# A decode attention kernel: two parts of the last V product as loops over a register

## The chip, the cores and the metric

The kernel runs on one core of a Trainium2 chip. The metric is device time in microseconds (us) of one execution, as the median of several runs. A profile is taken of one execution beside them; it lists the engines' instructions with start and length.

## The reference

Two attention blocks A and B, with the same shapes, each for two batches and a single query token. Their outputs are put side by side.

```
B, Sq, D = 2, 1, 640;  H, Sk, Dh = 32, 8192, 192
q      = (x @ wq) as [B, H, 1, Dh]
scores = einsum("bhqd,bhkd->bhqk", q, k_cache) * Dh ** -0.5
o      = einsum("bhqk,bhkd->bhqd", softmax(scores), v_cache)
out    = o as [B, 1, H * Dh] @ wo
result = concatenate([block A, block B], axis=-1)
```

All inputs are bf16. The K and V caches are most of the bytes: 2 blocks x 2 batches x 32 heads x 8192 tokens x 192 x 2 bytes, for K and for V.

## The kernel before

**Units and parts.** The work is cut into 16 units (`NU`) of one batch and 8 heads (`UH`). The K and the V of a unit are laid on 128 partitions, 16 partitions a head, and each partition has 512 tokens (`TP`) of 192 numbers. Each is loaded in three parts (`NCH`), of 170 whole tokens (`TC`) a partition and fragments of the two tokens that lie across the cuts. `big` has three buffers of one part each; the loads of all units go through them in a fixed order from SP's queue (`ld_kv`, L256), each one waiting until the part that was in its buffer is used up.

**A unit.** VectorE multiplies K with the query in place, TensorE sums over the head dimension with an identity matrix (`pe_sum`, `pe_rest`), VectorE reduces what is left. Then come the maximum, the exponential on ScalarE, and `dve_spread`, which writes the probabilities to `pb` as weights for TensorE. The V product of a unit runs on TensorE beside the K work of the next one.

**The V product** (`pe_pv(u, c)`, L450 in before) of part c takes two tokens a time: 85 products (`TC // 2`) with 40 columns of `pb` as weights (LDWEIGHTS, "PEld" in the profile) and 384 numbers of V a partition as the moving side, all added up in the PSUM tile `ops`. After the first of them come one or two small products for the fragments (L456). `pe_l` (L438) ahead of part 0 sums the exponentials.

**Loops.** `_Stream` holds each engine's instructions as a list, with a tag of slot and name; `emit` makes a hardware loop of slots that repeat, with addresses computed from the loop's register (`at`). Before, TensorE has three: two for the q projection (`pe_proj`, L402: 15 passes of five products of 384 columns each) and one for units 1 to 15, whose body has all 255 V products of a unit written out. A loop's own instructions have line L65.

**The tail.** After that loop comes the V product of the last unit, straight, with no K work beside it. What waits for it:
- When its part 0 is done, SP issues the load of A's output weights (`ld_wo`, L256) into that part's buffer; when part 1 is done, it issues B's in five pieces.
- When part 2 is done, VectorE and ScalarE scale the result (L349 to L358), `pe_pl` and `pe_turn` (L462, L471) turn it, and `pe_out` (L484) multiplies it with A's weights (96 products), then, after eight idle products (`pe_idle`, L492), with B's, piece by piece as they land.
- ScalarE and VectorE (L387, L388) write the sums to SBUF, and SP sends them out.

Of the kernel before, what the change touches and what calls it, by code (L numbers as in the profile page):

```python
# [119 lines left out]
def build_kernel(nc, blocks, out):  # L120
# [4 lines left out]
    UH = 8  # L125
    HG = Hn // UH
    NQB = NBLK * B
    NU = NQB * HG
    LASTU = NU - 1
    TP = Sk * UH // 128  # L130
    NCH = 3
    ROW = TP * Dh // NCH
    TC = ROW // Dh
    FR = ROW - TC * Dh
    OFF = (0, Dh - FR, FR)
# [8 lines left out]
    QW = 2 * Dh  # L144
# [3 lines left out]
    MP = HP + UH  # L148
    HM = Hn // 2
    XM = HM - 1  # L150
    PQ0 = -100
    XW = XM + 128
    PO = 128 - UH
    scale = float(Dh) ** -0.5
# [3 lines left out]
    with ExitStack() as es:  # L158
# [10 lines left out]
        pb = sb("pb", [128, TP * UH], BF16)  # L169
# [17 lines left out]
        rc = sb("rc", [UH, 1], F32)  # L187
# [10 lines left out]
        ops = ps("ops", [128, 512], F32)  # L198
# [8 lines left out]
        bufs = [big[:, i * ROW:(i + 1) * ROW] for i in range(NBUF)]  # L207
# [7 lines left out]
        S_pe = _Stream("pe", sem("s_pe"), reg, 1)  # L215
# [20 lines left out]
        buf = {}  # L236
# [43 lines left out]
        def fragments(b, c):  # L280
            if c == 0:
                return [(0, 0, FR, bufs[b][:, ROW - FR:ROW])]
            if c == 1:
                return [(0, FR, Dh, bufs[b][:, 0:Dh - FR]), (1, 0, Dh - FR, bufs[b][:, ROW - (Dh - FR):ROW])]
            return [(1, Dh - FR, Dh, bufs[b][:, 0:FR])]
# [154 lines left out]
        def col(s):  # L440
            return 64 * (s // 8) + 32 * (s % 2) + 8 * (s % 8 // 2)

        def pe_pv(u, c):
            b = buf["v", u, c]

            def fn(eng):
                for j in range(TC // 2):
                    j0 = col(TC * c + 2 * j)
                    last = c == NCH - 1 and j == TC // 2 - 1
                    ins = eng.matmul(ops[0:MP, 0:QW], pb[:, j0:j0 + MP],  # L450
                                     bufs[b][:, OFF[c] + j * QW:OFF[c] + (j + 1) * QW],
                                     start=(c == 0 and j == 0), stop=last, skip_group_check=True)
                    if j == 0:
                        for t, lo, hi, src in fragments(b, c):
                            j0 = col(NCH * TC + t)
                            eng.matmul(ops[0:UH, lo:hi], pb[:, j0:j0 + UH], src, start=False, stop=False,  # L456
                                       skip_group_check=True)
                return ins
            return fn

        def pe_pl(u):
            return lambda eng: eng.matmul(oacc_all[:, 0:Dh], place[:, S_pe.at(UH * u, 128, UH)], o_sb[:],  # L462
                                          start=False, stop=True, skip_group_check=True)
# [50 lines left out]
        for n in range(1, HP + 1):  # L514
            S_pool.add((lambda n: (lambda eng: eng.memset(tri[0:n, n:n + 1], 1.0)))(n),
                       waits=[("tri0",)] if n == 1 else [], sig=("tri",) if n == HP else None)
# [6 lines left out]
        for blk in range(NBLK):  # L523
            for b in range(B):
                S_dve.add(dve_xz(blk, b), waits=[("px",), ("init", 0)], sig=("xz",) if (blk, b) == (1, 1) else None)
        S_dve.add(lambda eng: eng.tensor_reduce(em[:], ident[:].rearrange("p (m t) -> p t m", t=GP), AXL.X, ALU.add),
                  waits=[("id1",)], sig=("em",))
        for i in range(GP):
# [3 lines left out]
                waits=[("em",), ("init", 2)], sig=("esel",) if i == GP - 1 else None)  # L532
        for i in range(HG):
# [3 lines left out]
                waits=[("init", 3)], sig=("onehot",) if i == HG - 1 else None)  # L537
        S_dve.add(lambda eng: eng.tensor_reduce(mask[:], ident[:].rearrange("p (h y) -> p h y", y=16), AXL.X, ALU.add),
                  sig=("mask",))
# [26 lines left out]

        streams = {"pe": S_pe, "dve": S_dve, "act": S_act, "pool": S_pool}
        slots = {e: {} for e in streams}

        def put(eng, slot, name, fn, waits, lag=0):  # L570
            slots[eng].setdefault(slot, []).append((name, fn, [w for w in waits if w is not None], lag))

        for u in range(NU + 1):
            real, old = u < NU, u >= 1
            v = u - 1

            def red(c, k):
                put("dve", u, ("r", c, k), dve_red(u, c, k), [("s", u, c, k), ("sp", u - 1) if u else None])

            def turn_out():  # L580
                put("dve", u, ("rc", -1), dve_rc, [("pv", v, NCH - 1), ("of", v - 1)])
                put("dve", u, ("oh", -1), dve_ohi, [("of", v - 1)])
                put("dve", u, ("os", -1), dve_osum, [("oh", v)])
                put("act", u, ("of", -1), act_of, [("os", v), ("rc", v), ("pl", v - 1)])

            def v_part(c):
                if c == 0:
                    put("pe", u, ("l", -1), pe_l, [("exp", v), ("sp0", v), ("os", v - 1), ("rc", v - 1)])
                put("pe", u, ("pv", c, -1), pe_pv(v, c), [("v", v, c), ("sp", v) if c else None])

            if not real:
                for c in range(NCH):
                    v_part(c)
                turn_out()
                put("pe", u, ("pl", -1), pe_pl(v), [("of", v)])
                continue
            put("dve", u, ("su", 1), dve_su(u + 1), [("q", u)])
            for c in range(NCH):
                if old:
                    v_part(c)  # L600
                for k in range(NSUB):
                    if old and c == NCH - 1 and k == 3:
                        turn_out()
                    w = [("k", u, c), ("qe", u), ("sl", u - 1, NCH - 1) if u and c == 0 else None]
                    put("dve", u, ("m", c, k), dve_mul(u, c, k), w)
                    put("pe", u, ("s", c, k), pe_sum(u, c, k), [("m", u, c, k), prev(u, c, k)])
                    if old and c == NCH - 1 and k == 3:
                        put("pe", u, ("pl", -1), pe_pl(v), [("of", v)])
                    n = NSUB * c + k - 3
                    if n >= 0:  # L610
                        red(n // NSUB, n % NSUB)
                put("pe", u, ("sl", c), pe_rest(u, c),
                    [("m", u, c, NSUB - 1), ("rl", u - 1) if u and c == 0 else None])
            c = NCH - 1
            for k in range(NSUB - 3, NSUB):
                red(c, k)
            put("dve", u, ("rl",), dve_rest, [("sl", u, c)])
            put("dve", u, ("mx",), dve_max, [("rl", u)])
            put("dve", u, ("mp",), dve_mp, [("mx", u), ("ar", u - 1) if u else None, ("negm",)])
            put("dve", u, ("nm",), dve_nm, [("ar", u)])  # L620
            put("dve", u, ("nb",), dve_nb, [("nm", u), ("exp", u - 1) if u else None])
            put("pe", u, ("q", 1), pe_q, [("su", u + 1), ("qe", u)])
            put("pool", u, ("ar",), pool_ar, [("mp", u), ("nm", u - 1) if u else None])
            put("act", u, ("qe", 1), act_q, [("q", u + 1), ("m", u, NCH - 1, NSUB - 1)])
            put("act", u, ("exp",), act_exp, [("nb", u), ("l", v) if u else None])
            g0, g1 = -(-TC // 8), TP // 8
            put("dve", u, ("sp0",), dve_spread([(0, g0), (g1 - 1, g1)]),
                [("exp", u), ("pv", v, NCH - 1) if u else None, ("mask",)])
            put("dve", u, ("sp",), dve_spread([(g0, g1 - 1)]), [])

        def full(name, u):
            lag = name[-1] if name[0] in ("su", "q", "qe", "l", "pv", "rc", "oh", "os", "of", "pl") else 0
            rest_ = name[1:-1] if lag else name[1:]
            return (name[0], u + lag) + rest_

        for e, S in streams.items():
            order = [n for n, *_ in slots[e][1]]
            have = {n for n, *_ in slots[e][0]}
            after = {}
            at = None  # L640
            for n in order:
                if n in have:
                    at = n
                else:
                    after.setdefault(at, []).append(full(n, 0))
            for u in sorted(slots[e]):
                for n, fn, waits, _ in slots[e][u]:
                    S.add(fn, waits=waits, sig=full(n, u), tag=(u, n),
                          pre=after.get(None, ()) if u == 0 and n == slots[e][0][0][0] else (),
                          post=after.get(n, ()) if u == 0 else ())  # L650

# [13 lines left out]
        with nc.Block() as block:  # L665
            @block.sync
            def _(eng):
                S_sp.emit(eng)

            @block.gpsimd  # L670
            def _(eng):
                S_pool.emit(eng)

            @block.vector
            def _(eng):
                S_dve.emit(eng, [(1, NU, 1)])

            @block.scalar
            def _(eng):
                S_act.emit(eng, [(1, NU, 1)])  # L680

            @block.tensor
            def _(eng):
                S_pe.emit(eng, [(PQ0 + 1, PQ0 + HM, 1), (PQ0 + 2 * HM + 1, PQ0 + 3 * HM, 1), (1, NU, 1)])

        for blk in range(NBLK):
            nc.scalar.wait_ge(*reg["odone", blk])
# [49 lines left out]
```

## Time and profile before

| what | value |
|---|---|
| median of 3 runs | 1937.39 us (1936.87 to 1938.21) |
| profiled execution, its own time | 1937.25 us |
| its span in the trace | 1935.4 us |
| TensorE (PE) busy | 1532.6 us, 79% |
| PE weight loads (PEld) busy | 784.1 us |
| VectorE (DVE) busy | 1119.2 us, 58% |
| DMA | 836.94 MB, mean 432 GB/s |

The span runs from the first instruction to the last; the execution's own time has 1.85 us more around it. "Busy" is the union of an engine's instructions. A matmul's length includes its way through the array, so products that follow each other every 0.16 us are listed with 0.33 each. "PEq" or "PEldq" is PE's sequencer, which computes addresses, branches, and hands instructions to the array. "issue" as a releaser means that an engine waited for nothing that the profile shows.

### The profile page before, as it was taken

The numbers are of one execution on the slowest core, as the hardware profiler recorded it, in microseconds if no ns is written. First come the engines' busy times: TensorE is split into PE (matmuls) and PEld (weight loads), VectorE is DVE, ScalarE is ACT, GpSimd is POOL, SyncE is SP. The second block draws the span as 40 slices with busy tenths as digits, with TensorE's granted clock in tenths as the row PEclk, the third lists the DMA queues.
The fourth block names the chain that finished last, engine by engine and source line by source line (L and its number), as shares of the span: only waits on it lengthen the run. The fifth ranks groups of instructions, "written<-read, shape, count | busy, mean of one in ns | idle before, by whom it ended". The sixth has DMA issues, their size and how long they took to land.

```text
span 1935.4 us, 18767 instructions
## 1 busy us (share of the span) xinstructions
PE 1532.6 (79%) x8255; PEld 784.1 (41%) x8256; DVE 1119.2 (58%) x841; ACT 29.6 (2%) x75; POOL 9.4 (0%) x60
## 2 busy tenths in 40 slices
PE   4778787887888778797787878878797777878778
PEld 2334343443434434353343434433343343434435
DVE  0785555846566485546846566485546846565450
ACT  0000000000000000000000000000000000000000
POOL 0000000000000000000000000000000000000000
PEclk9999898898999999999999999999998988999889
DMA  9999999999999999999999999999999999999998
GB/s 412 435 441 434 434 436 433 433 435 433 433 435 433 433 433 433 433 433 435 437 435 435 433 433 433 433 433 433 433 434 437 435 437 433 433 433 436 433 432 380
DMA packets 15147, 836.94 MB, mean 432 GB/s; under 512 B 1688, under 2 KB 1824, under 8 KB 2208
## 3 DMA queue, kind: packets, MB, share of 16 engines
q1 hardware_dynamic: 15136, 836.78, 99.8%
q8 instruction: 9, 0.15, 0.0%
q14 instruction: 2, 0.02, 0.0%
HBM read 836.77 MB, written 0.01 MB: 432 GB/s over the span
## 4 chain that ended last, share of the span: by engine, by line
PE 35%; DMA 34%; DVE 17%; issue 13%; DVEq 0%; POOL 0%; ACT 0%; SPq 0%; ACTq 0%; POOLq 0%
PE ops L450 22%; DMA big<-in_B_k_cache_dram 17%; DMA big<-in_A_k_cache_dram 14%; DVE big L305 12%; PE scps L420 10%; DVE sc L313 3%; DMA big<-in_B_wo_dram 2%; PE scps L402 2%; PE rest L432 1%; DMA pb<-in_B_x_dram 1%; DVE pb L340 1%; DVE rmax L321 0%; POOL mg L346 0%; PE ops L456 0%; DVE o_hi L352 0%
## 5 line engine op out<-in xcount | busy, mean ns | idle before, releaser
L420 PE MATMUL scps<-big,ident 128*128 128x512 bf16 x2880 | 716.5, 408 | 284.0 <-DVE sc L313 268.1
L305 DVE TENSOR_TENSOR big<-big,qt 128x6144 bf16<-128x6144 bf16 (+1 forms) x240 | 847.5, 3548 | 0.0
L450 PE MATMUL ops<-big,pb 128*40 128x384 bf16 x4080 | 710.7, 336 | 0.0
L420 PEld LDWEIGHTS scps<-big,ident 128*128 128x128 bf16 x2880 | 285.1, 103 | 700.6 <-DVE sc L313 332.9
L450 PEld LDWEIGHTS ops<-big,pb 128*40 128x40 bf16 x4080 | 414.5, 103 | 272.3 <-issue 28.9
L303 DVE TENSOR_TENSOR pad<-big,qt 128x128 bf16<-128x128 bf16 (+1 forms) x64 | 11.9, 207 | 633.7 <-DMA big<-in_B_k_cache_dram 341.5
L313 DVE TENSOR_REDUCE sc<-scps 128x32 f32<-128x512 f32 x240 | 161.0, 681 | 31.2 <-PE scps L420 31.2
L340 DVE TENSOR_TENSOR pb<-sc,mask 128x704 bf16<-128x704 f32 (+2 forms) x96 | 76.3, 863 | 14.1 <-ACT sc L367 14.1
L438 PE MATMUL ops<-rs,mask 128*8 128x1 f32 x32 | 3.1, 167 | 84.8 <-DVE pb L340 84.8
L432 PEld LDWEIGHTS rest<-big,ident 128*128 128x128 bf16 x576 | 44.4, 101 | 13.9 <-issue 4.5
L432 PE MATMUL rest<-big,ident 128*128 128x160 bf16 x576 | 49.1, 236 | 0.0
L438 PEld LDWEIGHTS ops<-rs,mask 128*8 128x8 f32 x32 | 1.6, 90 | 88.4 <-DVE pb L340 82.8
L402 PE MATMUL scps<-big,pb 128*128 (+1 forms) x160 | 31.7, 338 | 6.8 <-issue 6.8
L358 ACT ACTIVATE o_sb<-o_hi,rc 8x192 bf16<-8x192 f32 x16 | 7.3, 454 | 1537.2 <-DVE o_hi L355 1537.2
L349 DVE RECIPROCAL rc<-ops 8x1 f32<-8x1 f32 x16 | 2.3, 147 | 41.4 <-PE ops L450 41.4
L295 DVE TENSOR_TENSOR su<-esel,onehot 128x144 bf16<-128x144 bf16 x17 | 5.1, 300 | 35.8 <-PE outps L410 35.8
L402 PEld LDWEIGHTS scps<-big,pb 128*128 (+1 forms) x160 | 15.7, 99 | 22.6 <-issue 15.1
L395 PE MATMUL rest<-ident,pb 4*128 4x4 bf16 x5 | 0.4, 178 | 21.9 <-DMA pb<-in_B_x_dram 21.9
L346 POOL PARTITION_ALL_REDUCE mg<-mp x16 | 5.8, 365 | 1855.2 <-DVE mp L324 1855.2
L317 DVE TENSOR_REDUCE sc<-rest 128x30 f32<-128x480 f32 x16 | 10.5, 657 | 7.3 <-PE rest L432 7.3
L367 ACT ACTIVATE sc<-sc,nb 128x512 f32<-128x512 f32 x16 | 11.5, 721 | 32.8 <-DVE nb L330 32.8
L292 DVE CAST pb<-rest 128x5 bf16<-128x5 f32 x4 | 0.4, 171 | 19.5 <-PE rest L395 19.5
(66 smaller groups left out, 131.5 us busy)
## 6 DMA issues: line engine op xcount, KB each, us to landing
big<-in_B_wq_dram SPq DMA_DIRECT2D x1, 7680.0 KB, 37.4
big<-in_A_wo_dram SPq DMA_DIRECT2D x1, 7680.0 KB, 29.2
big<-in_A_wq_dram SPq DMA_DIRECT2D x1, 7168.0 KB, 20.3
big<-in_B_wo_dram SPq DMA_DIRECT2D x1, 4640.0 KB, 27.7
big<-in_B_wo_dram SPq DMA_DIRECT2D x1, 1760.0 KB, 31.4
big<-in_B_wo_dram SPq DMA_DIRECT2D x1, 800.0 KB, 32.8
big<-in_A_wq_dram SPq DMA_DIRECT2D x1, 512.0 KB, 3.8
big<-in_A_k_cache_dram SPq DMA_DIRECT2D x24, 38.4
```

Source lines behind the costliest of these rows:

```text
L303: eng.tensor_tensor(pad[:, t, lo:hi], src, qt[:, 0, lo:hi], ALU.mult)
L305: return eng.tensor_tensor(t, t, qt[:].broadcast_to([128, size(k), Dh]), ALU.mult)
L313: return lambda eng: eng.tensor_reduce(sc[:, lo:lo + SUB], scps[bank(u, c, k)][:], AXL.X, ALU.add)
L317: eng.tensor_reduce(dst, rest[:, 0:NCH * REST, :].rearrange("p (c t) g -> p c t g", c=NCH), AXL.X, ALU.add)
L340: ins = eng.tensor_tensor(dst[:, lo:hi, a], src[:, lo:hi, a].unsqueeze(3).broadcast_to(shape), mask[:].unsqueeze(1).unsqueeze(1).broadcast ...
L346: return eng.partition_all_reduce(mg[:], mp[:], 128, bass.bass_isa.ReduceOp.max)
L358: return eng.activation(o_sb[:], o_hi[:], ACTF.Identity, scale=rc[:])
L367: return eng.activation(sc[:], sc[:], ACTF.Exp, bias=nb[:], scale=scale, accum_out=rs[:])
L402: ins = eng.matmul(flat[0][:, 0:QW], xz[:, blk, c, S_pe.at(m, 128)], wq_t[blk][:, c, S_pe.at(QW * m, QW, QW)], start=(blk == 0 and m == 0 ...
L420: ins = eng.matmul(scps[bank(u, c, k)][:], ident[:], t[:, :, j * DG:(j + 1) * DG], start=(j == 0), stop=(j == NJ - 1))
L432: ins = eng.matmul(rest[:, lo:lo + n, :], ident[:], src[:, :, j * DG:(j + 1) * DG], start=(j == 0), stop=(j == NJ - 1))
L450: ins = eng.matmul(ops[0:MP, 0:QW], pb[:, j0:j0 + MP], bufs[b][:, OFF[c] + j * QW:OFF[c] + (j + 1) * QW], start=(c == 0 and j == 0), stop= ...
```

## The change

For the last unit alone, parts 0 and 1 of the V product are written as loops. The first product and the fragments of a part stay ahead of its loop (`pe_pv_head`); the other 84 products are 21 passes (`VN`) of four (`VP`). Both operands' addresses are taken from the loop's register: 64 columns of `pb` and 1536 of V a pass. Each pass ends with a semaphore update; who waited for the part's end now waits for that of its last pass. Part 2 and the units in the main loop stay as they were.

```diff
+    PV0 = 1000
+    VP = 4
+    VN = (TC // 2 - 1) // VP
...
+        def pe_pv_head(u, c):
+            b = buf["v", u, c]
+
+            def fn(eng):
+                j0 = col(TC * c)
+                ins = eng.matmul(ops[0:MP, 0:QW], pb[:, j0:j0 + MP], bufs[b][:, OFF[c]:OFF[c] + QW],
+                                 start=(c == 0), stop=False, skip_group_check=True)
+                for t, lo, hi, src in fragments(b, c):
+                    j0 = col(NCH * TC + t)
+                    ins = eng.matmul(ops[0:UH, lo:hi], pb[:, j0:j0 + UH], src, start=False, stop=False,
+                                     skip_group_check=True)
+                return ins
+            return fn
+
+        def pe_pv_pass(u, c, i):
+            b = buf["v", u, c]
+
+            def fn(eng):
+                for n in range(VP):
+                    j = 1 + VP * i + n
+                    ins = eng.matmul(ops[0:MP, 0:QW], pb[:, S_pe.at(col(TC * c + 2 * j), MP, 16 * VP)],
+                                     bufs[b][:, S_pe.at(OFF[c] + j * QW, QW, VP * QW)],
+                                     start=False, stop=True, skip_group_check=True)
                 return ins
             return fn
...
             if not real:
+                put("pe", u, ("l", -1), pe_l, [("exp", v), ("sp0", v), ("os", v - 1), ("rc", v - 1)])
                 for c in range(NCH):
-                    v_part(c)
+                    if c == NCH - 1:
+                        put("pe", u, ("pv", c, -1), pe_pv(v, c), [("v", v, c)])
+                        continue
+                    put("pe", u, ("pvh", c), pe_pv_head(v, c), [("v", v, c), ("sp", v) if c else None])
+                    for i in range(VN):
+                        n = ("pv", c, -1) if i == VN - 1 else ("pvt", c, i)
+                        put("pe", u, n, pe_pv_pass(v, c, i), [])
+                        tags["pe", u, n] = (PV0 + 100 * c + i, ("pvt", c))
...
-                S_pe.emit(eng, [(PQ0 + 1, PQ0 + HM, 1), (PQ0 + 2 * HM + 1, PQ0 + 3 * HM, 1), (1, NU, 1)])
+                S_pe.emit(eng, [(PQ0 + 1, PQ0 + HM, 1), (PQ0 + 2 * HM + 1, PQ0 + 3 * HM, 1), (1, NU, 1)]
+                          + [(PV0 + 100 * c, PV0 + 100 * c + VN, 1) for c in range(NCH - 1)])
```

How TensorE's instructions stand in the tail, first in before, from the sum of the exponentials (L438) to the placing of the result (L462):

```order
L438 MATMUL ops<-rs,mask 8x1
L450 MATMUL ops<-big,pb 40x384
L456 MATMUL ops<-big,pb 8x128
L450 MATMUL ops<-big,pb 40x384 x85
L456 MATMUL ops<-big,pb 8x64 x2
L450 MATMUL ops<-big,pb 40x384 x85
L456 MATMUL ops<-big,pb 8x128
L450 MATMUL ops<-big,pb 40x384 x84
L462 MATMUL oall<-o_sb,place 128x192
```

There 84 products of part 0 and the first of part 1 stand in a row, then the fragments, and the same again for parts 1 and 2. After the change, TensorE's loop of part 0 (ISA is an address step on PE's sequencer; lines from L110 on are later in the file than before):

```order
L65 UNCONDITIONAL_BRANCH
L65 ISA
L485 ISA
L485 MATMUL ops<-big,pb 40x384
L485 ISA
L485 MATMUL ops<-big,pb 40x384
L485 ISA
L485 MATMUL ops<-big,pb 40x384
L485 ISA
L485 MATMUL ops<-big,pb 40x384
L65 REGISTER_ALU
L65 COMPARE_AND_BRANCH
```

The 84 products have become one body of four that is passed 21 times, with an address step ahead of each and three sequencer steps a pass. The end of the second loop on TensorE and what follows it, after the change:

```order
L65 REGISTER_ALU
L65 COMPARE_AND_BRANCH
L454 MATMUL ops<-big,pb 40x384
L460 MATMUL ops<-big,pb 8x128
L454 MATMUL ops<-big,pb 40x384 x84
L492 MATMUL oall<-o_sb,place 128x192
```

Part 2 (L454, L460) is as it was, and stands right behind the loop's branch.

More of the change, by code (lines that the diff above doesn't have):

```diff
@@ L151, in build_kernel @@
     PQ0 = -100
+    PV0 = 1000
+    VP = 4
+    VN = (TC // 2 - 1) // VP
+    assert VP % 4 == 0 and 1 + VN * VP == TC // 2
     XW = XM + 128
@@ L459, in pe_pv @@
             return fn
+        def pe_pv_head(u, c):
[18 more added lines that the diff above has]
+                                     start=False, stop=True, skip_group_check=True)
+                return ins
+            return fn
         def pe_pl(u):
@@ L568, in build_kernel @@
         slots = {e: {} for e in streams}
+        tags = {}
         def put(eng, slot, name, fn, waits, lag=0):
@@ L647, in build_kernel @@
                 for n, fn, waits, _ in slots[e][u]:
-                    S.add(fn, waits=waits, sig=full(n, u), tag=(u, n),
+                    S.add(fn, waits=waits, sig=full(n, u), tag=tags.get((e, u, n), (u, n)),
                           pre=after.get(None, ()) if u == 0 and n == slots[e][0][0][0] else (),
```

## The prediction

> **What bounds the kernel now.** I read the page's head first, then the chain that ended last, then the tail of the timeline.
>
> ```profile
> span 1935.4 us, 18767 instructions
> PE 1532.6 (79%) x8255; PEld 784.1 (41%) x8256; DVE 1119.2 (58%) x841; ACT 29.6 (2%) x75; POOL 9.4 (0%) x60
> DMA packets 15147, 836.94 MB, mean 432 GB/s; under 512 B 1688, under 2 KB 1824, under 8 KB 2208
> ```
>
> 836.94 MB at 432 GB/s is the whole span: up to the last unit the loads are the bound, and TensorE waits for data. The change touches nothing there. It sits in the last 67 us, where the chain of waits (start, length, what) reads:
>
> ```profile
> 1869.26 15.33 PE ops L450 x85
> ...
> 1884.74 13.77 PE ops L450 x84
> ...
> 1898.53 0.33 SPq L256
> ...
> 1899.38 32.77 DMA big<-in_B_wo_dram
> ...
> 1932.19 1.46 PE scps L484 x16
> ...
> 1933.68 0.48 DVE pb L388
> ```
>
> The two V parts of the change (L450) stand on the chain themselves. The end of part 1 releases SP's issue of the second weight matrix (L256), its landing releases the last output products (L484), and these end the kernel. The timeline of the same stretch shows how much slack the neighbours have:
>
> ```profile
> 1869.19 15.40 PE L450 MATMUL ops<-big,pb 128*40 128x384 bf16 x85
> ...
> 1871.73 0.16 PEld L450 LDWEIGHTS ops<-big,pb 128*40 128x40 bf16 x1 [0.16 <-issue]
> 1872.05 12.14 PEld L450 LDWEIGHTS ops<-big,pb 128*40 128x40 bf16 x75 [0.16 <-issue]
> 1884.45 0.33 SPq L256 DMA_DIRECT2D big<-in_A_wo_dram  x1
> ...
> 1898.53 2.24 SPq L256 DMA_DIRECT2D big<-in_B_wo_dram  x5
> ...
> 1898.74 13.83 PE L450 MATMUL ops<-big,pb 128*40 128x384 bf16 x84
> 1912.60 0.16 DVE L349 RECIPROCAL rc<-ops 8x1 f32<-8x1 f32 x1 [41.44 <-PE ops L450]
> ...
> 1915.58 8.36 PE L484 MATMUL outps<-big,oT 128*2 128x320 bf16 x96
> ...
> 1924.10 1.67 PE L492 MATMUL ops<-big,ident 128*128 128x512 bf16 x7 [0.16 <-issue]
> ...
> 1926.27 5.69 PE L484 MATMUL scps<-big,oT 128*2 128x320 bf16 x80 [0.50 <-DMA big<-in_B_wo_dram]
> ...
> 1932.19 1.45 PE L484 MATMUL scps<-big,oT 128*2 128x320 bf16 x16 [0.23 <-DMA big<-in_B_wo_dram]
> ```
>
> PE has no hole from 1869.19 to 1912.60, and the last output products wait for the DMA by only 0.50 and 0.23 us. DMA and PE end almost together, so whatever lengthens PE's V product moves the end after about a microsecond.
>
> **What a looped pass costs.** No product goes away. 168 of the 255 straight V products become two loops of 21 passes with four products each. A pass adds four address instructions (one ahead of each product), a register step, a branch, and one more address instruction behind the branch. Before has a loop of the same build: the q projection (L402), 15 passes of five products with the same 384 columns.
>
> ```profile
> L402 PEldq FUSED_REGOPS  x150: 42/74/84, 23.1 to 60.3; - x150
> ...
> L65 PEldq COMPARE_BRANCH  x45: 83/215/238, 23.9 to 1862.3; - x45
> ```
>
> Minimum, median and maximum in ns: 150 address instructions (one a product) of 74 ns, and a taken branch of 215 ns, all on PE's sequencer. What they do to the products stands in the timeline of PE and of its weight loads:
>
> ```profile
> 22.78 6.49 PE L402 MATMUL scps<-big,pb 128*128 128x384 bf16 x30 [0.53 <-issue]
> ...
> 29.52 0.73 PEld L402 LDWEIGHTS scps<-big,pb 128*128 x5 [0.53 <-issue]
> ```
>
> ```profile
> 30.79 0.98 PE L402 MATMUL scps<-big,pb 128*128 x5 [0.27 <-issue]
> 32.05 0.98 PE L402 MATMUL scps<-big,pb 128*128 x5 [0.28 <-issue]
> ...
> 40.88 3.50 PE L402 MATMUL scps<-big,pb 128*128 x20 [0.26 <-issue]
> 44.64 0.98 PE L402 MATMUL scps<-big,pb 128*128 x5 [0.26 <-issue]
> ...
> 59.78 0.50 PE L402 MATMUL scps<-big,pb 128*128 x2 [0.27 <-issue]
> ```
>
> ```profile
> 34.00:38.00 4.00, 3.17 (x17) 1.46 (x16) 0.00 (x0) 0.00 (x0) 0.00 (x0) 1.00 1.13 492
> ```
>
> From 30.79 to 59.78 lie 23 passes: 28.99 / 23 = 1.260 us for five products, though at the full clock (1.00 in the third fence's window) a straight product needs 12.14 us / 75 = 0.162 (weight loads from 1872.05), so 0.81 for five. Nothing is waited for ("issue"): the sequencer paces the loop. Within a pass the weight loads follow each other by (0.73 - 0.10) / 4 = 0.158 us, 0.10 being one load; between passes PE's weight loader idles 0.53. So a pass of four is 1.260 - 0.158 = 1.10 us against 4 x 0.162 = 0.65 straight. This value I take. Its bounds from the same rows: 1.26 if the fifth product was free beside the sequencer, 1.26 x 4/5 = 1.01 if everything scales. The step from one loop to the next costs a pass: 40.88 to 44.64 is three passes of 1.25, though five straight products and a loop entry lie in it.
>
> **Part 0.** Before: first product of the 84 at 1869.19, issue of A's weights at 1884.45. After: the 21st pass starts at 1869.19 + 20 x 1.10 = 1891.19, its fourth product 3 x 0.158 later at 1891.67, and with 0.34 for the product itself the issue comes at 1892.0, 7.6 us late. The cold start of before (0.32 us apart until 1872.05, about nine products) does not come on top: 4 x 0.32 = 1.28 lasts three passes at most, and the sequencer is ahead of PE by then, as in the 30 gapless products from 22.78. At most 0.4 us. What hides the late issue is the V part 2 load ahead of it in the queue:
>
> ```profile
> big<-in_A_wo_dram SPq DMA_DIRECT2D x1, 7680.0 KB, 29.2
> ...
> big<-in_A_wq_dram SPq DMA_DIRECT2D x1, 512.0 KB, 3.8
> ```
>
> The last column is us from issue to landing. 7680 KB (7.86 MB) at 432 GB/s are 18.2 us, so of A's 29.2 us 11.0 are spent behind V part 2, until 1884.45 + 11.0 = 1895.5. The first load of all took 3.8 us of which 1.2 move 512 KB, so a start costs at most 2.6: 1892.0 + 2.6 = 1894.6 is still in time. Cost nothing; A lands at about 1913.7 as before.
>
> **Part 1.** Its first pass starts one pass after loop 0's last: 1869.19 + 21 x 1.10 = 1892.29; its 21st at 1914.29, last product 0.48 later, done at 1915.1. There the five DMAs of B's weights are issued, 16.6 us later than 1898.53. Now the cover is gone: A has landed at 1913.7, the DMA engines run dry for about 4 us, and B (7680 KB too) lands at 1915.1 + 2.6 + 18.2 = 1935.9 at the latest.
>
> **Part 2 and the tail.** Part 2 stays straight: 14.07 us from 1898.53 to 1912.60, so the reciprocal comes at 1929.2, and with some 0.1 for leaving the loop 1929.3, 16.7 late. Everything to the eighth idle product moves along; before, that one ended at 1924.10 + 8 x 0.214 = 1925.8, now at 1942.5 (0.214 is 1.67 less the 0.38 of the last, over six steps). B has then been in SBUF for 6.6 us, so the last 96 products run without a wait: 40 pairs took 5.69 with 0.1 of waiting and a last one of 0.30, thus 0.136 a pair, 48 pairs 6.5, and 0.2 until the last is read. They end at 1949.2 instead of 1933.65 (1932.19 + 1.45), 15.5 later: the 16.7 less 1.2 of waits for B that vanish. Behind them nothing changes. Fewer fetches of instructions (320 instructions fewer) weigh nothing where PE is the bound. The gate on PE's clock can add or take one slow window:
>
> ```profile
> 1916.00:1920.00 4.00, 4.00 (x40) 2.19 (x36) 0.00 (x0) 0.00 (x0) 0.00 (x0) 0.57 0.94 408
> ```
>
> Clock 0.57 after the 3 us pause around 1914 cost output products some 1.7 us; I leave it in, as the pause stays.
>
> The profiled execution took 1937.25 us for its 1935.4 span, 0.14 under the median of 1937.39. 1937.25 + 15.5 = 1952.8 us, 0.8% slower. Each 0.01 us on a pass is 0.41 us here.
>
> **Rivals.**
> The other side, *the sequencer runs ahead*: if PE's queue held enough products, the address work would be hidden and nothing moves. For it: 30 products from 22.78 to 29.3 without a gap. Against it: those began at half clock, and when the lead was spent every one of 23 passes showed the gap. It decides below a pass of 0.82 us: the tail may then slip by 1.2 + 3.9 (0.2% of the time, about what a measurement of this kernel can tell from no change) = 5.1 against 16.7, and 11.6 / 41 = 0.28 off 1.10. Fully hidden it gives 1936 to 1937. Chance 5%.
> *Only the branch shows*: address instructions lie beside the products, and a pass costs 0.65 + 0.215 = 0.865. Shift 16.7 - 41 x 0.235 = 7.1, less 1.2: 1943.1 us. Against it: 0.53 of idling where the branch explains 0.215. Chance 4%.
> The Trainium skill, "Advanced Engine Details and Errata", section "Control Flow Timing", states about 108 ns for a compare-and-branch; by that alone an estimated pass is 0.76 us and the time about 1939. The row says 215 for a taken one, and the measurement decides.
> *The clock halves in the loops*: PE's array works 0.65 of each 1.10. If the gate closed, four products at 0.32 make 1.28 a pass: 41 x 0.18 = 7.4 more, 1960.2. Against it: clock 1.00 through the five-product loop, at 0.81 of 1.26. Chance 4%.
> *B's landing ends it*: 6.6 us too early for that; 1%.
>
> **How the numbers follow.** The likeliest, with 86%, is 1952.8. The range takes a pass from 1.00 to 1.20, that is -4.1 to +4.1, with a little below for a sequencer that is quicker when no profile is taken: 1948.0 to 1957.0; the upper bound of 1.26 (1959.4) I leave out, because the spacing of loads shows each product costing its 0.158. Faster by over 0.2%: 1%, since the DMA floor leaves nothing to win. Within 0.2%: 4%. Slower: 95%.
>
> **What would show it.** In the profile after: L485 products in groups of four, 1.10 us apart, with 0.4 us of "issue" between; A's issue near 1892, B's near 1915; a dent in GB/s near 1916; the reciprocal near 1929; last products without a DMA wait. The prediction is wrong if the passes come closer than 0.82 us, or if TensorE's clock in the loops is not 1.00.

## The result and the profile after

The changed kernel took 1952.76 us (median of 6 runs, 1950.94 to 1954.72), the kernel before 1937.16 us (6 runs, 1936.75 to 1938.21). The ratio is 1.0081, 95% interval 1.0068 to 1.0094: 0.8% slower.

The profiled execution took 1954.72 us, the longest of its six. The head of its page, to be held against that of before:

```profile
span 1953.0 us, 19063 instructions
PE 1544.1 (79%) x8255; PEld 784.2 (40%) x8256; DVE 1119.6 (57%) x841; ACT 29.6 (2%) x75; POOL 9.4 (0%) x60
```

The engines do the same work (x8255 products in both); 296 more instructions pass through the sequencers, and the span is 17.6 us longer. The tail of its timeline (start, length, engine, what, count, idle before it and its releaser), TensorE first and then the rows of other engines and the end:

```profile
1870.89 4.92 PE L485 MATMUL ops<-big,pb 128*40 x20
1876.08 0.86 PE L485 MATMUL ops<-big,pb 128*40 x4 [0.28 <-issue]
1877.21 0.82 PE L485 MATMUL ops<-big,pb 128*40 x4 [0.28 <-issue]
...
1892.85 0.86 PE L485 MATMUL ops<-big,pb 128*40 x4 [0.28 <-issue]
...
1894.13 0.83 PE L485 MATMUL ops<-big,pb 128*40 x4
1895.21 0.82 PE L485 MATMUL ops<-big,pb 128*40 x4 [0.25 <-issue]
...
1916.47 0.82 PE L485 MATMUL ops<-big,pb 128*40 x4 [0.32 <-issue]
```

```profile
1893.74 0.33 SPq L260 DMA_DIRECT2D big<-in_A_wo_dram  x1
...
1917.33 2.59 SPq L260 DMA_DIRECT2D big<-in_B_wo_dram  x5
...
1931.47 0.16 DVE L353 RECIPROCAL rc<-ops 8x1 f32<-8x1 f32 x1 [58.61 <-PE ops L454]
...
1934.44 8.36 PE L514 MATMUL outps<-big,oT 128*2 128x320 bf16 x96
...
1942.96 1.67 PE L522 MATMUL ops<-big,ident 128*128 128x512 bf16 x7 [0.16 <-issue]
...
1944.56 6.68 PE L514 MATMUL scps<-big,oT 128*2 128x320 bf16 x96
```

Three things are to be seen here. The looped products come in fours, with 0.28 us of "issue" between: 15 passes from 1876.08 to 1892.85 are 1.118 us each. The issue of B's weights has moved from 1898.53 to 1917.33. And the last 96 output products run in one row without a wait for B, where before they stood in two with waits: the last piece of B's weights landed at 1939.21 us in the trace, and the first of these products starts at 1944.56. TensorE ends this kernel alone.

The clock that was granted to TensorE in the two loops, and the load between them, stand in the windows (the last three numbers are the clock, the busy share of the DMA engines, and GB/s):

```profile
1884.00:1892.00 8.00, 6.00 (x30) 2.79 (x30) 0.00 (x0) 0.00 (x0) 0.00 (x0) 1.00 0.96 418
...
1896.00:1912.00 16.00, 11.58 (x58) 5.38 (x57) 0.00 (x0) 0.00 (x0) 0.00 (x0) 1.00 0.98 426
1912.00:1916.00 4.00, 3.12 (x16) 1.50 (x16) 0.00 (x0) 0.00 (x0) 0.00 (x0) 1.00 0.04 15
```

The clock was full (the first loop's first 2.6 us, up to 1873.5, were at half clock, as the start of this tail was in before), and behind A's weights the DMA engines ran dry.

The whole tail of this execution lies 1.70 us later than that of before from its first product on (L442 at 1870.13 against L438 at 1868.43), and this lateness arises ahead of the changed code: the tails of e1 and e4, which have loops too, start at 1868.46 and 1868.40 (see the section on the hardware). Where start times are compared below, they are taken from the tail's own start.

### The profile page after: what moved, and what is told of

It is laid out like the page before. It is cut to its first block, busy times and chain, and to the rows that moved or that the text cites. A ratio compares the mean times of both kernels' runs of the same rounds, so it can differ in the third digit from the quotient of the medians.

```text
span 1953.0 us, 19063 instructions
## 1 busy us (share of the span) xinstructions
PE 1544.1 (79%) x8255; PEld 784.2 (40%) x8256; DVE 1119.6 (57%) x841; ACT 29.6 (2%) x75; POOL 9.4 (0%) x60
## 4 chain that ended last, share of the span: by engine, by line
PE 35%; DMA 34%; DVE 18%; issue 13%; DVEq 0%; POOL 0%; ACT 0%; SPq 0%; ACTq 0%; POOLq 0%
PE ops L454 20%; DMA big<-in_A_k_cache_dram 19%; DMA big<-in_B_k_cache_dram 14%; DVE big L309 13%; PE scps L424 9%; DVE sc L317 3%; PE ops L485 2%; PE scps L406 2%; PE rest L436 1%; DMA pb<-in_B_x_dram 1%; DVE pb L344 1%; DVE rmax L325 0%; PE outps L514 0%; PE scps L514 0%; POOL mg L350 0%
## 5 line engine op out<-in xcount | busy, mean ns | idle before, releaser
L454 PE MATMUL ops<-big,pb 128*40 128x384 bf16 x3910 | 679.5, 335 | 0.0
L454 PEld LDWEIGHTS ops<-big,pb 128*40 128x40 bf16 x3910 | 396.5, 102 | 259.9 <-issue 25.8
L442 PE MATMUL ops<-rs,mask 128*8 128x1 f32 x32 | 3.2, 168 | 84.8 <-DVE pb L344 84.8
L485 PE MATMUL ops<-big,pb 128*40 x168 | 35.6, 338 | 10.4 <-issue 10.4
L442 PEld LDWEIGHTS ops<-rs,mask 128*8 128x8 f32 x32 | 1.6, 90 | 88.4 <-DVE pb L344 82.8
L485 PEld LDWEIGHTS ops<-big,pb 128*40 x168 | 16.5, 99 | 29.1 <-issue 21.5
```

The costliest lines, as they stand in the source:

```text
L454: ins = eng.matmul(ops[0:MP, 0:QW], pb[:, j0:j0 + MP], bufs[b][:, OFF[c] + j * QW:OFF[c] + (j + 1) * QW], start=(c == 0 and j == 0), stop= ...
L485: ins = eng.matmul(ops[0:MP, 0:QW], pb[:, S_pe.at(col(TC * c + 2 * j), MP, 16 * VP)], bufs[b][:, S_pe.at(OFF[c] + j * QW, QW, VP * QW)], s ...
```

## The experiments

Theory: PE's sequencer paces the loop, at 0.51 us a pass and 0.1525 us a product, and since TensorE is then late, its lateness passes to the end. The rivals put the cost on the array (a fixed 0.47 us a pass with products at their own pace), make both loops cost the same, or let B's landing end the kernel. All times are medians; "before" ran on the same chip each time and stood at 1937.1 to 1937.3.

**e1: 7 passes of 12 products.**

```diff
-    VP = 4
+    VP = 12
```

> Both loops with 7 passes of 12 products in place of 21 of 4. Theory (PE's sequencer paces the loop, a pass is 0.51 us plus 0.1525 us a product, read off the 1.119 us pass of the looped kernel): a pass of 2.34 us, part 0 about 0.5 us late (the half-clocked start gives the sequencer a lead), part 1 about 2.5 us late, 1938.5 us. Rival (each pass costs a fixed 0.47 us on the array and products keep their 0.1625 us): a pass of 2.42 us from the first pass on, B's weights issued 5.7 us late, 1941.7 us.

Measured: 1939.86 us (1937.17 to 1941.02, 10 runs), ratio 1.0013, interval 1.0003 to 1.0022. The timeline of PE:

```profile
1869.21 13.50 PE L485 MATMUL ops<-big,pb 128*40 x72
1882.94 2.12 PE L485 MATMUL ops<-big,pb 128*40 x12 [0.23 <-issue]
...
1887.77 2.12 PE L485 MATMUL ops<-big,pb 128*40 x12 [0.20 <-issue]
...
1899.51 2.12 PE L485 MATMUL ops<-big,pb 128*40 x12 [0.24 <-issue]
...
1901.66 2.23 SPq L260 DMA_DIRECT2D big<-in_B_wo_dram  x5
```

Five passes from 1887.77 to 1899.51 make 2.348 us, the theory's 2.34 and not 2.42. The first 72 products show no gap, so the lead of the half-clocked start lasted six passes. With the four-product pass the two terms come apart: (2.348 - 1.118) / 8 = 0.154 us a product, 1.118 - 4 x 0.154 = 0.50 us a pass. B's weights are issued 33.20 us after the start of this tail (1868.46), against 30.10 in before: 3.1 us late, where the theory had 2.5 and the rival 5.7.

The sequencer's own records in the looped kernel (minimum, median and maximum in ns) show a part of the 0.50:

```profile
L485 PEldq FUSED_REGOPS  x168: 51/74/79, 1870.4 to 1916.8; - x168
...
L65 PEldq FUSED_REGOPS  x87: 50/78/83, 22.4 to 1916.2; - x87
L65 PEldq ALU_OP  x87: 32/36/42, 23.3 to 1917.0; - x87
L65 PEldq COMPARE_BRANCH  x87: 83/215/238, 23.4 to 1917.1; - x87
```

The taken branch (215 ns), the register step (36) and the address step behind the branch (78) make 0.33 us. The remaining 0.17 lie between these steps; no run parts them further.

The time itself lies between theory (1938.5) and rival (1941.7), because its spread of 3.9 us is as large as their distance; the lines decide.

**e2 and e3: one part alone as a loop.** The other one stands straight, as before.

```diff
-                    if c == NCH - 1:
+                    if c != 0:          # e2;  e3: if c != 1
```

> Only part 0 is a loop, part 1 straight. Theory: part 0's last product comes 7.9 us late (its half-clocked start costs nothing on top of the loop), B's issue 7.9 us late but still before A's weights have landed, so the DMA engines do not run dry; the end moves by 7.9 less the 1.2 us that the last products had waited for B: 1943.9 us. Rival (both loops cost the same): half of the 15.6 us, 1945.0 us. Rival (the end goes by B's landing, which cannot come later here): 1937.5 us.

> Only part 1 is a loop, part 0 straight. Theory: no half-clocked start covers it, part 1's last product comes 9.6 us late, 1945.6 us, 1.7 us more than with part 0 alone. Rival (both loops cost the same): 1945.0 us. Rival (the end goes by B's landing, at most 0.5 us late): 1937.7 us.

Measured: e2 1943.36 us (1941.77 to 1945.34, 7 runs), ratio 1.0032 (1.0020 to 1.0043); e3 1944.12 us (1942.32 to 1944.73, 6 runs), ratio 1.0032 (1.0019 to 1.0044). Both rule out that B's landing ends the kernel. Of the other two forecasts, the times alone decide nothing: e2's runs spread over both the theory's 1943.9 and the rival's 1945.0, and e3's median is nearer to the rival's 1945.0 than to the theory's 1945.6. In the lines, e2's part 0 (A's issue 23.59 us after the start of its tail, 16.02 in before) comes 7.6 us late, where the theory had 7.9. e3's time is 1.5 us shorter than the theory said; its timeline shows why:

```profile
1886.17 0.33 SPq L260 DMA_DIRECT2D big<-in_A_wo_dram  x1
...
1886.38 4.08 PE L485 MATMUL ops<-big,pb 128*40 x24
1890.77 0.82 PE L485 MATMUL ops<-big,pb 128*40 x4 [0.31 <-issue]
...
1907.27 2.23 SPq L260 DMA_DIRECT2D big<-in_B_wo_dram  x5
```

24 products, six passes, run without a gap at the full clock. From A's issue to B's are 21.10 us; in the looped kernel, where part 0's loop stands ahead, they are 1917.33 - 1893.74 = 23.59. (In time it shows as 1.5 us and not as these 2.5; the profiled execution of e3 began its tail 1.8 us late, at 1870.24, as that of the looped kernel did.) The sequencer had entered the loop early: its first loop instruction stands at 1883.6 us in the trace, 2.8 us ahead of the loop's first product, while TensorE still had some 14 straight products to do. So a loop behind straight code seems to start with a lead: its first products are already handed out while TensorE works through the straight ones. My "no cover" for part 1 alone was wrong; e8 tests this.

**e4: the looped kernel without the eight idle products.**

```diff
-            if n == 0:
-                S_pe.add(pe_idle, waits=[("of", LASTU)])
```

> The looped kernel without the eight idle products ahead of the last 96 output products. Theory (the tail is bound by TensorE, B has landed over 5 us before it is used): the last products start 1.73 us earlier, 1951.0 us. Rival (the late landing of B's weights ends the kernel): no change, 1952.8 us.

Measured: 1950.69 us (1949.02 to 1950.80, 4 runs), ratio 1.0066 (1.0049 to 1.0083). In before the idle products hide in the wait for B; here they come off the end: 2.07 us between the medians, where 1.73 were expected. The ratios of this kernel and the looped one have overlapping intervals, so the time alone does not decide, and the timeline does:

```profile
1932.71 8.09 PE L514 MATMUL outps<-big,oT 128*2 128x320 bf16 x96
...
1940.63 6.68 PE L514 MATMUL scps<-big,oT 128*2 128x320 bf16 x96
```

B's products start while the pipeline still empties of A's (1932.71 + 8.09 = 1940.80), without a wait for DMA; the last piece of B's weights landed at 1937.37 in this trace. TensorE is the bound of the looped tail.

**e5: 3 passes of 28 products.**

```diff
-    VP = 4
+    VP = 28
```

> Both loops with 3 passes of 28 products. Theory (a pass is 0.51 us plus 0.1525 us a product on PE's sequencer): 4.78 us a pass against 4.55 us of products; part 0 not late at all, part 1 about 0.3 us late, less than the 1.2 us by which the last products wait for B's weights: 1937.0 us, no change within 0.5 us. Rival (a fixed 0.47 us a pass on the array): B's issue 1.9 us late, 1937.9 us. Rival (fewer fetches of instructions relieve the DMA engines that land last): 1935.7 us.

Measured: 1937.09 us (1936.86 to 1937.81, 11 runs) against 1937.32; ratio 0.9999 (0.9990 to 1.0008).

```profile
1869.23 15.41 PE L485 MATMUL ops<-big,pb 128*40 x84
...
1884.88 13.83 PE L485 MATMUL ops<-big,pb 128*40 x84
```

Both loops run as one row, within 0.2 us of straight code (15.40 for 85 products from 1869.19 and 13.83 for 84 in before), and B's weights are issued 30.27 us after the tail's start, against 30.10: the array rival's 1.9 us are not there. What cost 0.8% is not that there are loops, but that the fixed part of a pass came with every four products. A pass of 28 is not free for the sequencer, though: at 0.50 + 28 x 0.154 it is 4.81 us against 4.55 for the products, and here a lead hides the difference (e9 shows the same loop without one).

**e6 and e7: the same loops with products of half the columns.**

```diff
-                    ins = eng.matmul(ops[0:MP, 0:QW], ...,  bufs[b][:, S_pe.at(OFF[c] + j * QW, QW, VP * QW)],
+                    ins = eng.matmul(ops[0:MP, 0:Dh], ...,  bufs[b][:, S_pe.at(OFF[c] + j * QW, Dh, VP * QW)],
```

> The looped kernel with the loops' products cut to 192 of their 384 columns (half of the V product of parts 0 and 1 is left out). Theory (the sequencer paces the loop): a pass stays at 1.12 us, B's issue and the time stay as with 384 columns, 1952.8 us. Rival (products at the array's pace and 0.47 us a pass on top): a pass of 0.47 + 4 x 0.081 = 0.79 us, B's issue 13.5 us earlier than with 384 columns, under 1940 us.

> The loops with 7 passes of 12 products, each cut to 192 of its 384 columns (half of the V product of parts 0 and 1 is left out). With e6 it gives the two terms of a pass apart, since the array needs only 0.081 us a product. Theory: 0.51 + 12 x 0.1525 = 2.34 us a pass, so 0.1525 us a product and 0.51 us a pass. Rival (array and a fixed 0.47 us): 0.47 + 12 x 0.081 = 1.44 us.

Measured, one run each: e6 1952.73 us, e7 1940.83 us, as long as their wide twins (1952.76 and 1939.86). The clock spoils e6 as a proof; here are the windows of e6 and then of e7 (the number ahead of the last two is the granted clock):

```profile
1876.00:1891.00 15.00, 11.03 (x55) 5.66 (x54) 0.00 (x0) 0.00 (x0) 0.00 (x0) 0.50 0.98 424
```

```profile
1876.00:1891.00 15.00, 12.95 (x82) 7.59 (x80) 0.00 (x0) 0.00 (x0) 0.00 (x0) 0.99 0.99 428
```

In e6 TensorE stayed at half clock, so half the columns took as long as all of them at the full one (0.16 us a product, estimated as half of the 0.32 that 384 columns take at half clock in before), and the array rival (0.47 + 4 x 0.16 = 1.11) fits too. e7 ran at 0.99, and its passes:

```profile
1877.59 1.96 PE L485 MATMUL ops<-big,pb 128*40 x12 [0.38 <-issue]
...
1884.68 1.96 PE L485 MATMUL ops<-big,pb 128*40 x12 [0.41 <-issue]
```

Three passes from 1877.59 to 1884.68 make 2.363 us each, though by the estimate of 0.081 us a product the array needed 0.97. Within a pass the products follow each other by 0.155 us ((1.96 - 0.255) / 11, the length of one being 0.255). That it is not the weight loads which hold them apart is shown by a row of straight products in before, each with a load of 128 columns of weights:

```profile
1861.59 0.99 PE L432 MATMUL rest<-big,ident 128*128 128x160 bf16 x12
```

These stand some 0.07 us apart ((0.99 - 0.24) / 11). So e7 shows that the sequencer sets the pace; the rival's 1.44 is out.

**e8: 16 straight products between the two loops.** Part 0 has 17 passes of four, then its last 16 products straight.

```diff
+                    passes = VN if c else VN - 4
-                    for i in range(VN):
+                    for i in range(passes):
...
+                    if passes < VN:
+                        put("pe", u, ("pv", c, -1), pe_pv_rest(v, c, 1 + VP * passes), [])
```

> As the looped kernel, but part 0 has 17 passes of four and its last 16 products stand straight between the two loops. Part 1 alone as a loop (e3) had come out 2.5 us shorter than part 1 behind the loop of part 0: 21.1 us between the issues of A's and B's weights against 23.6. Theory (while TensorE works through straight products its sequencer runs some 14 products ahead, and the next loop lives on that lead): 21.2 us between the issues, B's issue 42.9 us after the start of the tail, 1948.8 us. Rival (a loop of 21 passes costs the same wherever it stands, and e3 was short for another reason): 23.6 us between the issues, 1951.1 us.

Measured: 1947.99 us (1947.01 to 1948.27, 4 runs), ratio 1.0057 (1.0041 to 1.0072).

```profile
1887.49 2.77 PE L485 MATMUL ops<-big,pb 128*40 128x384 bf16 x16
...
1890.50 4.08 PE L496 MATMUL ops<-big,pb 128*40 x24
1894.76 0.82 PE L496 MATMUL ops<-big,pb 128*40 x4 [0.18 <-issue]
```

Between the issues of A's weights (1890.29) and B's (1911.25) lie 20.96 us, the theory's 21.2, though a loop stands ahead in part 0. Sixteen straight products (2.77 us of work) gave the second loop its six gapless passes back. The lead is shown.

**e9, e10, e11: can a looped version win?** e9 has 7 passes of 12 in part 0, 3 of 28 in part 1, and no idle products. e10 is e9 with six products on data of no use behind part 2, which keep TensorE at work while it waits for the scaled result. e11 is the kernel before with the six in place of its eight idle ones.

```diff
+            for i in range(6):
+                ins = eng.matmul(flat[0], ident[:], v2[:, 512 * i:512 * (i + 1)], start=True, stop=True)
```

> Part 0 in 7 passes of 12 products, part 1 in 3 passes of 28, and no idle products: a version that may beat both, since part 0's lateness of 0.5 us is covered by the load ahead of A's, and the shorter program moves the last fetch of instructions (at 1930.3 us in e5, with two pieces of B's weights landing 0.9 us late behind it) past the last landing. Theory: last piece lands near 1932.4 instead of 1933.3 and the end comes 0.9 us earlier, 1936.3 us. Rival (the last landing does not go by that fetch, or TensorE is behind by then): 1937.2 us or a little more.

> As e9 (7 passes of 12, 3 passes of 28), with six products of 512 columns on data of no use right behind part 2, in the 1.5 us in which TensorE waits for the scaled result. In e9 the half-clocked stretch after that pause made A's 96 output products 9.5 us long where 6.7 are enough, so TensorE and not the landing ended the kernel. Theory: the gate stays open, A's products take 6.7 us, and the last piece's landing near 1932.1 sets the end: 1935.7 us, and the spread of the runs gets smaller. Rival (the gate closes all the same, or e9's median was chance): 1936 to 1937.2 us.

> The kernel before, straight in all parts, with the same six products behind part 2 in place of the eight idle ones. Theory (what e9 and e10 win is the earlier last landing, from the shorter program): A's output products take 6.7 us in place of 8.4, but they then wait longer for B's weights, which land at 1933.3 as in the kernel before: 1937.2 us. Rival (the open gate alone brings the gain): as fast as e10.

Measured: e9 1935.93 us (1935.78 to 1938.53, 11 runs), ratio 0.9995 (0.9986 to 1.0004). e10 1935.68 us (1935.53 to 1936.00, 11 runs) against 1937.13 (1936.68 to 1938.19, 21 runs), ratio 0.9992 (0.9983 to 1.0001). e11 1937.59 us (1937.05 to 1938.53, 11 runs), ratio 1.0002 (0.9993 to 1.0011). The second loop and the output products of e9, then the output products of e10 and of e11:

```profile
1885.59 14.41 PE L486 MATMUL ops<-big,pb 128*40 x84
...
1917.15 9.49 PE L515 MATMUL outps<-big,oT 128*2 128x320 bf16 x96
1926.48 6.69 PE L515 MATMUL scps<-big,oT 128*2 128x320 bf16 x96
```

```profile
1916.83 6.68 PE L515 MATMUL outps<-big,oT 128*2 128x320 bf16 x96
...
1924.59 5.83 PE L515 MATMUL scps<-big,oT 128*2 128x320 bf16 x80 [1.08 <-DMA big<-in_B_wo_dram]
1930.68 1.57 PE L515 MATMUL scps<-big,oT 128*2 128x320 bf16 x16 [0.26 <-DMA big<-in_B_wo_dram]
```

```profile
1916.84 6.68 PE L484 MATMUL outps<-big,oT 128*2 128x320 bf16 x96
...
1926.04 8.28 PE L484 MATMUL scps<-big,oT 128*2 128x320 bf16 x96 [2.51 <-DMA big<-in_B_wo_dram]
```

The second loop of e9 has 3 passes of 28 as in e5, but stands behind a loop of 12 that had used up its lead (in the timeline, that loop's last two passes have gaps of 0.26 and 0.21 us ahead of them). It took 14.41 us where straight code and e5 have 13.83: without a lead, 28 products a pass still cost 0.6 us in this part.

With the granted clock at 1.00 throughout, A's products take 6.68 us, and e10's last products end at 1932.25, where the kernel before ends at 1933.64: B's pieces land 1.3 us earlier (the last at 1931.90 us in e10's trace, at 1933.22 in e11's and 1933.29 in that of before; e10 and e11 both issued B's weights at 1899.78). e11 has the same full clock in A's products and no gain: its B products then ran at half clock from 1925.92 to 1929.34, but its last landing alone lies 1 us behind the end of e10's. So the clock alone does not bring the gain. e10's runs all lie below all of before's, though the interval of the ratio just touches 1. The gain of 0.07% is at the edge of what these runs can tell.

Why B lands earlier is not settled. In seven profiles the last landing was near 1931.9 with two fetches of PE instructions (16 KB each) in the tail ahead of it (e1, e3, e10; in e10 a third began 0.4 us before the landing) and near 1933.2 with three (before, e5, e11), but e2 had two and 1933.2. That the fetches hold up the landing fits most, and not all.

## Why the prediction was right

- **How near the time came.** Forecast 1952.8 us, measured 1952.76. That is nearer than the working can claim: the runs lie 3.8 us apart, and the profiled one began its tail 1.70 us late for a reason that the prediction does not have. What the runs bear out is the working below, to about half a microsecond.
- **What bounds the tail.** Right. Lateness of the V product went to the end less the waits for B; e2, e3 and e4 show it part by part.
- **The pass of 1.10 us.** It was 1.118, 0.018 a pass short: the sum took the q projection's pass less one product, and over 41 passes that would make 0.7 us. Its premise, that address steps and branch pace the loop and products bring 0.158 each, holds with 0.154 and 0.50 (e1, e7).
- **Part 0: A's issue 7.6 us late.** 1893.74 less the late start of 1.70 is 1892.04; predicted 1892.0. The half-clocked start costs nothing on top, as said. That it agrees to 0.04 us is luck: the first five passes ran without a gap, at 1.04 us each (1870.89 to 1876.08), and the other fifteen at 1.118, which nearly makes the predicted 1.10 on average.
- **"A lands at about 1913.7 as before."** In e4, whose tail starts on time, yes (1913.56 us in the trace). In the profile of the changed kernel the late start ate the 1 us of spare cover, and A landed at 1914.77, 1.2 us later; nothing waited for it. With the 18.1 us that A takes behind the landing of V part 2 in e4 (1895.45 to 1913.56), its start took an estimated 2.9 us there, where the sum had 2.6 at most.
- **Part 1: B's issue at 1915.1.** 1917.33 - 1.70 = 1915.63. The reciprocal at 1931.47 - 1.70 = 1929.77, predicted 1929.3; the end of the last products at 1951.24 - 1.70 = 1949.54, predicted 1949.2. Of the 0.5 us at B's issue, the passes of the second loop make 0.34 (20 x 0.017), and the step from one loop to the next, 1.28 us (1892.85 to 1894.13) where the sum had a pass of 1.10, the rest.
- **"B lands at 1935.9 at the latest."** This bound was too low: in e4, whose tail starts on time, the last piece landed at 1937.37 us, 21.8 us after the first one's issue where the sum had 20.8. In the looped kernel 5.3 us were left until B's products began, not 6.6. It changed nothing, since nothing waited for B.
- **The rivals.** "The sequencer runs ahead" holds after all where it has a lead, at the head of a loop behind straight code (24 products in e3 and e8), and for 84 products when a pass has 28 (e5). It did not decide here because the lead lasted for 20 products of the first loop, and the second loop stood right behind it with none. "Only the branch shows" fell: a pass costs 0.50 beside its 0.154 a product, the taken branch 0.215 of it. The Trainium skill, "Advanced Engine Details and Errata", section "Control Flow Timing", has 108 ns for the branch: half of what is measured here, and a fifth of a pass's fixed part. "The clock halves in the loops" did not happen with four wide products (1.00 in the windows above); in e6, with narrow ones, it stayed at 0.50.
- **Not seen:** the spread. The runs of the changed kernel lie 3.8 us apart, those of before 1.5.

## What to carry to other kernels

A loop over a register on TensorE is paced by its sequencer when a pass is short: by these runs, price it as 0.50 us a pass and 0.154 us a product with an address step, and compare with the products' own 0.1625 us (384 columns at the full clock). With four products a pass it cost 70% on top; with 28 it cost nothing where there was a lead (e5), and 0.6 us on 84 products where there was none (e9). Sequencer time is hidden only by a lead: straight products ahead of the loop gave about 2.5 us of it (e3, e8), and two short loops in a row had none for the second. In a tail where DMA and TensorE end within a microsecond, look at which of them has slack before lengthening either.

## What the runs showed of the hardware

**The clock gate makes executions differ.** The granted clock of TensorE stands at 1.00 or at 0.50 (the gate is open or closed). The K products and the window of time from 1859.87, well ahead of the changed code, in before and then after the change:

```profile
1858.99 2.76 PE L420 MATMUL scps<-big,ident 128*128 128x512 bf16 x12 [1.92 <-DVE sc L313]
...
1859.87:1863.29 3.42, 3.18 (x35) 2.00 (x33) 1.33 (x3) 0.13 (x1) 0.00 (x0) 1.00 0.93 402
```

```profile
1859.00 4.45 PE L424 MATMUL scps<-big,ident 128*128 128x512 bf16 x12 [1.92 <-DVE sc L317]
...
1859.87:1863.29 3.42, 3.42 (x10) 1.21 (x9) 0.27 (x1) 0.00 (x0) 0.00 (x0) 0.50 0.84 364
```

At half clock 12 K products took 4.45 us where they took 2.76, and the tail began 1.7 us later, though the last part of V landed at the same time (1895.49 and 1895.44 us). The other place is A's output products: 6.68 us in e1, where the clock stays at 1.00; 8.36 in the looped kernel, where it is 0.50 from 1934.97 to 1938.38; 9.49 in e9, where it is 0.50 from 1916.09 to 1922.91. A kernel that ends on DMA would hide most of both; one that ends on TensorE would show them, and 2 x 1.7 us are most of the 3.8 between its runs. No trace of the other runs is kept, so that this makes their spread is argued and not shown.

**Short gaps alone neither open the gate nor keep it open.** In e6 no gap between products was over 0.3 us, yet the clock stayed at 0.50 for 51 us, through both loops and 3.4 us of the straight part 2: at half clock, 4 products of some 0.16 us (estimated above) in 1.11 us are 58% of the time. In the looped kernel the same 58% (4 x 0.162 of 1.118) at full clock kept it at 1.00. And in e7, where 12 products at an estimated 0.081 us fill 41% of a pass, the clock held for 20.5 us and then fell to 0.50 for one window in the midst of the loop, with no gap over 0.41 us:

```profile
1876.40:1896.88 20.48, 17.28 (x107) 9.96 (x106) 0.00 (x0) 0.00 (x0) 0.00 (x0) 1.00 1.00 433
1896.88:1900.29 3.41, 3.13 (x20) 2.02 (x19) 0.00 (x0) 0.00 (x0) 0.00 (x0) 0.50 1.12 486
```

So the same 58% kept a full clock full and a halved one halved, and 41% kept it full only for a time. These are single executions, and no run measures the bounds. The Trainium skill, "TensorE: Matmul & The Clock Gate", section "Why this matters for your kernels", asks for no idle gap over about 3 us between bursts, to avoid drops in the middle of a kernel. e7 shows a drop without such a gap.
